# Retention attention and a gated feed-forward in one kernel: the first eight chunks taken head by head with zero-padded operands, output stores issued on the load queue, and later weights loaded in 2 KB pieces

## The chip, the cores and the metric

The kernel runs on one core of one Trainium2 chip. The metric is the device time in microseconds (us) of one execution; shorter is better. TensorE is called PE below, its weight loads PEld, VectorE DVE, ScalarE ACT, GpSimd POOL, and SyncE, which here only issues DMAs, SP.

## The reference

Eight batches with eight heads of 576 positions and 64 features go through a retention attention (causal, without softmax, with a decay per head). Its output, seen as 4608 tokens of 512 features, goes through a feed-forward of width 1536 with a sigmoid gate.

```python
scores = q @ k^T / sqrt(64)
gamma  = 1 - 2 ** (-5 - head)
Dmat   = gamma ** (i - j) where i >= j, else 0
x      = ((scores * Dmat) @ v)            # heads side by side: (4608, 512)
out    = ((sigmoid(x @ w_gate)) * (x @ w_val)) @ w_out
```

Inputs and output are float32; the kernel computes its matmuls in bfloat16 with float32 sums.

## The kernel before

**Attention by chunks.** Each batch of 576 positions is cut into five chunks of 128, 128, 128, 128 and 64 positions; with eight batches that makes 40 steps, counted by s. The decay is split: keys are multiplied by gamma^-pos (`ks`, on POOL, line 197), queries by gamma^pos / sqrt(64) (`qs`, line 200), so that inside a chunk only a causal mask is left. A step has four phases. Phase t (line 216) turns keys and queries so that features lie on the partitions: for the first eight steps (`EARLY = 8`) by eight PE transposes into one PSUM tile `tr`, from which ACT copies `qT` (line 230) and DVE copies the keys into `kbd` (line 235); for later steps by two DMA transposes issued on SP (line 207), from which DVE copies `kbd`. Phase qk (line 240) multiplies; two heads share one matmul, because `kbd` and `vbd` hold two heads of 64 positions as a block diagonal in one 128x128 tile, and DVE multiplies the result by the mask `tri` (line 254, or 261 for a half chunk). Phase st (line 286) adds the chunk's keys times values to a state, which DVE masks with `bdm` (`sb`, line 304). Phase pv (line 265) sums state times queries and `vbd` times masked scores, and ACT copies the result to `xT` (line 284), the transposed input of the feed-forward.

**Preparation of a step.** `cast(s)` (line 178) writes the values twice in bfloat16: plainly as `vn`, and as four quarter blocks into `vbd`, by ACT for the first eight steps (line 189), by POOL later (line 191). `load(s)` (line 73) issues three DMAs of 256 KB for values, keys and queries (128 KB for a half chunk), in rows of 256 bytes.

**Feed-forward.** A unit is four matmuls `h` (line 351) for one of twelve feature blocks fc; ACT applies the sigmoid to the gate unit (`g`, line 356) and DVE multiplies (`gv`, line 360). Three PSUM tiles serve all units. When all twelve are there, twelve matmuls `op` (line 372) give 128 tokens of output, ACT copies them to `ob` (line 377) and issues the store on its own DMA queue (line 379). The first block has 512 tokens and is written out by hand (`first_units`, line 404), since it grows while steps 0 to 3 are computed and weights arrive. Then come blocks of 128, of 256, seven of 512 and one of 128 tokens.

**What sets the order.** Each engine runs its instructions in the order of the program. A list (line 310) gives the phases; `advance` (line 390) places them between feed-forward units. At phase t of step s the program first issues `load(s + 6)` and casts all steps up to s + 2 (only step s itself while s < 4), see line 329:

```python
while done["cast"] < min(NS, s + (1 if s < 4 else LEAD_CAST)):
```

**Loads.** All loads and DMA transposes are on SP's queue: steps 0 and 1, weights for fc 0 and 1, step 2, weights for fc 2 to 5, step 3, the other gate and value weights, twelve tiles of `w_out`, then steps 4, 5 and on. Gate and value weights come as tiles of two row blocks by 256 columns (1 KB rows), `w_out` in 2 KB rows. The 22 buffers of `ld` serve them all; a buffer comes free when its cast is done. Beside that, the DMAs share eight completion semaphores in turn, so that a DMA waits for one that stood eight places before it, whichever queue it is on.

Of the kernel before, what the change touches and what calls it, by code (L numbers as in the profile page):

```python
# [9 lines left out]
FP32 = mybir.dt.float32  # L10
# [6 lines left out]
def kernel(  # L17
# [22 lines left out]
    P = 128  # L40
# [6 lines left out]
    ld_pool = ctx.enter_context(tc.tile_pool(name="ld", bufs=22))  # L47
# [4 lines left out]
    osb_pool = ctx.enter_context(tc.tile_pool(name="osb", bufs=3))  # L52
# [14 lines left out]
    EARLY = 8  # L67

# [15 lines left out]
    def load_w(f):  # L84

        for nm, src in (("g", moe_w_gate), ("v", moe_w_val)):
            for i in range(2):
                t = ld_pool.tile([P, 2, 2 * P], FP32, tag="ld", name=f"w{nm}32_{f}_{i}")
                nc.sync.dma_start(
                    out=t, in_=src[i * 2 * P:(i + 1) * 2 * P, f * P:(f + 2) * P].rearrange("(c p) f -> p c f", p=P))  # L90
                parts[nm, f, i] = t
# [36 lines left out]
    nc.scalar.activation(out=qtab, in_=arg, func=AF.Exp, bias=lnscale, scale=1.0)  # L128

# [3 lines left out]
    for i in range(NB):  # L133
        nc.vector.memset(vbd[i], 0.0)
        if i < 3:
            nc.gpsimd.memset(kbd[i], 0.0)

    tri = consts.tile([P, 192], BF16)  # L140
    nc.gpsimd.memset(tri, 1.0)
    for p0 in (0, 64):
        for c0 in (0, 128):
            nc.gpsimd.affine_select(
                out=tri[p0:p0 + 64, c0:c0 + 64], in_=tri[p0:p0 + 64, c0:c0 + 64],
                compare_op=ALU.is_ge, fill=0.0, base=0,
                pattern=[[1, 64]], channel_multiplier=-1)
    bdm = consts.tile([P, P], BF16)
    nc.gpsimd.memset(bdm, 0.0)
    nc.gpsimd.memset(bdm[0:64, 0:64], 1.0)  # L150
    nc.gpsimd.memset(bdm[64:128, 64:128], 1.0)
# [6 lines left out]
    def cast_w(f):  # L158
        for i in range(2):
            nc.gpsimd.tensor_copy(out=wg_sb[:, 2 * i:2 * i + 2, f * P:(f + 2) * P], in_=parts.pop(("g", f, i)))  # L160
            if i == 0:
                nc.vector.tensor_copy(out=wv_sb[:, 0:2, f * P:(f + 2) * P], in_=parts.pop(("v", f, 0)))
            else:
                nc.scalar.copy(out=wv_sb[:, 2:4, f * P:(f + 2) * P], in_=parts.pop(("v", f, 1)))

    def cast_wo(f):
        if f % 2:
# [313 lines left out]
```

## Time and profile before

| what | value |
|---|---|
| time, median of 3 runs (lowest to highest) | 375.67 us (375.01 to 377.22) |
| time of the profiled execution | 378.67 us |
| its span, first to last instruction | 377.0 us |
| mean granted PE clock | 0.968 of full |
| PE busy | 338.5 us (90%) |
| ACT, DVE, POOL busy | 140.7, 170.9, 154.2 us |
| DMA moved | 55.11 MB, 146 GB/s over the span |

A row of the windows view gives a stretch of the span, its length, then for each engine the busy time and the number of instructions, the granted PE clock, the busy share of the 16 DMA engines and the rate. A timeline row gives start and length of an instruction or a group of like ones, and in brackets how long the engine had been idle and what ended that. A row by line gives the total, the mean in ns of one, and the idle time ahead of the group.

### The profile page before, as it was taken

Reading aid. Unit: us, or ns where it says so; the run is one execution under the profiler, and the core shown is the slowest. Engines: PE = TensorE matmul, PEld = TensorE weight load, DVE = VectorE, ACT = ScalarE, POOL = GpSimd, SP = SyncE. Lnnn points to the kernel's source line nnn. Section 1 sums busy time; section 2 is a strip of 40 time slices with the busy share of each in tenths; the row PEclk is TensorE's granted clock in tenths of the full one; section 3 lists DMA queues with packets and bytes.
Section 4 is the critical chain, followed back from the end, with each engine's and each line's share of the span. In section 5 each row is a group of like instructions: output and inputs, shape, how many; then the busy total and the mean of one; then the engine's idle time right before and its main releaser. Section 6 shows DMA issues by size and latency. Waiting matters only on the chain.

```text
span 377.0 us, 6771 instructions
## 1 busy us (share of the span) xinstructions
PE 338.5 (90%) x2464; PEld 189.7 (50%) x2464; DVE 170.9 (45%) x353; ACT 140.7 (37%) x280; POOL 154.2 (41%) x254
## 2 busy tenths in 40 slices
PE   1668994679896999999999999999999999999996
PEld 0554741366763555555555555554555455544454
DVE  4645551145772545264346425651663266324212
ACT  5646466333431232333233324332332333233232
POOL 6424331347692466444636572553444470000000
PEclk9868997889999899999999999999999999999999
DMA  9999998697999979866865798569532310110020
GB/s 177 296 298 360 285 214 172 131 202 135 179 190 200 183 150 183 185 99 134 188 155 113 139 231 133 113 125 237 99 70 59 111 30 16 56 57 2 28 85 29
DMA packets 157218, 55.11 MB, mean 146 GB/s; under 512 B 144896, under 2 KB 151040, under 8 KB 157184
## 3 DMA queue, kind: packets, MB, share of 16 engines
q1 hardware_dynamic: 152000, 45.24, 59.9%
q10 hardware_dynamic: 5184, 9.44, 8.4%
q8 instruction: 19, 0.31, 0.4%
q14 instruction: 15, 0.12, 0.1%
HBM read 37.75 MB, written 9.44 MB: 125 GB/s over the span
## 4 chain that ended last, share of the span: by engine, by line
PE 81%; ACT 7%; DMA 4%; DVE 4%; POOL 2%; issue 2%; ACTq 0%; SPq 0%; POOLq 0%; DVEq 0%
PE h L351 48%; PE op L372 21%; PE pv L283 5%; DVE kbd L235 3%; PE qk L250 2%; ACT vbd L189 2%; PE st L295 2%; DMA out_dram<-ob 2%; DMA k<-in_k_dram 1%; ACT ob L377 1%; ACT qT L230 1%; PE qk L252 1%; DMA v<-in_v_dram 1%; ACT vn L189 1%; PE tr L226 1%
## 5 line engine op out<-in xcount | busy, mean ns | idle before, releaser
L360 DVE TENSOR_TENSOR gv<-g,h 128x512 bf16<-128x512 bf16 (+3 forms) x142 | 79.2, 559 | 101.7 <-PE h L351 71.0
L351 PE MATMUL h<-xT,wv_sb 128*128 128x512 bf16 (+3 forms) x568 | 118.7, 332 | 5.3 <-ACT g L356 5.3
L351 PE MATMUL h<-xT,wg_sb 128*128 128x512 bf16 (+3 forms) x568 | 119.4, 334 | 3.3 <-ACT xT L284 3.0
L356 ACT ACTIVATE g<-h 128x512 bf16<-128x512 f32 (+3 forms) x142 | 69.9, 495 | 127.6 <-PE h L351 116.8
L372 PE MATMUL op<-wo_sb,gv 128*128 128x512 bf16 x432 | 102.3, 387 | 0.0
L191 POOL CAST vbd<-v 64x256 bf16<-64x256 f32 x114 | 45.1, 396 | 111.6 <-PE pv L283 107.9
L351 PEld LDWEIGHTS <-wg_sb 128*128 128x128 bf16 x568 | 51.8, 100 | 46.0 <-issue 4.8
L351 PEld LDWEIGHTS <-wv_sb 128*128 128x128 bf16 x568 | 49.6, 100 | 39.9 <-issue 7.1
L372 PEld LDWEIGHTS <-gv 128*128 128x128 bf16 x432 | 41.1, 99 | 45.5 <-issue 2.5
L254 DVE TENSOR_TENSOR pt<-qk,tri 128x384 bf16<-128x384 f32 x64 | 32.7, 552 | 43.9 <-PE qk L252 43.9
L197 POOL TENSOR_TENSOR ks<-k,ktab 128x512 bf16<-128x512 f32 (+1 forms) x40 | 41.6, 1040 | 15.8 <-DMA k<-in_k_dram 12.1
L377 ACT COPY ob<-op 128x512 f32<-128x512 f32 x36 | 21.1, 585 | 68.6 <-PE op L372 57.0
L200 POOL TENSOR_TENSOR qs<-q,qtab 128x512 bf16<-128x512 f32 (+1 forms) x32 | 33.4, 1044 | 0.0
L284 ACT CAST xT<-pv 128x512 bf16<-128x512 f32 (+1 forms) x40 | 21.7, 542 | 30.5 <-PE pv L283 30.5
L250 PE MATMUL qk<-qT,kbd 128*128 128x128 bf16 x128 | 15.8, 225 | 11.9 <-DVE kbd L235 11.9
L304 DVE TENSOR_TENSOR sb<-st,bdm 128x512 bf16<-128x512 f32 x32 | 22.0, 688 | 9.6 <-PE st L295 9.6
L283 PE MATMUL pv<-pt,vbd 128*128 128x64 bf16 (+1 forms) x288 | 25.1, 213 | 0.2 <-DVE pt L254 0.2
L283 PEld LDWEIGHTS <-vbd 128*128 128x128 bf16 x288 | 21.3, 103 | 5.8 <-issue 1.4
L191 POOL CAST vn<-v 128x512 bf16<-128x512 f32 (+1 forms) x32 | 19.6, 612 | 9.1 <-PE st L295 4.1
L235 DVE COPY kbd<-kT 64x512 bf16<-64x512 bf16 (+1 forms) x64 | 21.3, 333 | 1.6 <-DMA kT<-ks 0.6
L250 PEld LDWEIGHTS <-kbd 128*128 128x128 bf16 x128 | 11.9, 100 | 17.0 <-DVE kbd L235 14.4
L283 PE MATMUL pv<-qT,sb 128*128 128x128 bf16 (+1 forms) x128 | 19.6, 220 | 0.0
(42 smaller groups left out, 150.0 us busy)
## 6 DMA issues: line engine op xcount, KB each, us to landing
out_dram<-ob ACTq DMA_DIRECT2D x36, 256.0 KB, 2.9
v<-in_v_dram SPq DMA_DIRECT2D x32, 256.0 KB, 4.0
k<-in_k_dram SPq DMA_DIRECT2D x32, 256.0 KB, 4.4
q<-in_q_dram SPq DMA_DIRECT2D x32, 256.0 KB, 5.0
wg<-in_moe_w_gate_dram SPq DMA_DIRECT2D x12, 256.0 KB, 4.8
wv<-in_moe_w_val_dram SPq DMA_DIRECT2D x12, 256.0 KB, 5.6
wo<-in_moe_w_out_dram SPq DMA_DIRECT2D x12, 256.0 KB, 5.6
v<-in_v_dram SPq DMA_DIRECT2D x8, 128.0 KB, 3.7
```

The lines of the kernel that those rows point to most:

```text
L191: nc.gpsimd.tensor_copy(out=o, in_=i)
L197: nc.gpsimd.tensor_tensor(out=ks[0:n], in0=k32[0:n], in1=ktab[0:n, c, :].unsqueeze(2).to_broadcast([n, H, D]), op=ALU.mult)
L200: eng.tensor_tensor(out=qs[0:n], in0=q32[0:n], in1=qtab[0:n, c, :].unsqueeze(2).to_broadcast([n, H, D]), op=ALU.mult)
L235: nc.vector.tensor_copy(out=kb[p0:p0 + 64, 0:nj, :, p0:p0 + 64].rearrange("p j m t -> p m j t"), in_=kT[p0:p0 + 64, 0:M, 0:n].rearrange("p ...
L250: nc.tensor.matmul(qkp[:, mm, 0:128], lhsT=kb[:, 0, m, :], rhs=qT[:, m, 0:128], start=True, stop=True)
L254: nc.vector.tensor_tensor(out=pt[:, 2 * g:2 * g + 2, :], in0=qkp[:, :, 0:192], in1=tri.unsqueeze(1).to_broadcast([P, 2, 192]), op=ALU.mult)
L283: nc.tensor.matmul(pvp[:, m, a:e], lhsT=w, rhs=x, start=(i == 0), stop=(i == len(mm) - 1))
L351: nc.tensor.matmul(hp[:, a:e], lhsT=w_sb[:, kc, fc * P:(fc + 1) * P], rhs=xT[:, kc, t0 + a:t0 + e], start=(kc == 0), stop=(kc == NKC - 1))
L356: nc.scalar.activation(out=g[:, a:e], in_=hp[:, a:e], func=AF.Sigmoid)
L360: nc.vector.tensor_tensor(out=gvs[fc][:, a:e], in0=gate[:, a:e], in1=hp[:, a:e], op=ALU.mult)
L372: nc.tensor.matmul(opp, lhsT=gvs[fc][:, nb * P:(nb + 1) * P], rhs=wo_sb[:, fc, :], start=(fc == 0), stop=(fc == NFC - 1))
L377: nc.scalar.copy(out=ob, in_=opp)
```

## The change

It has four parts that stand in the same diff.

- **Head by head.** For steps 0 to 7, values and keys go into `vpad` and `kpad`, tiles with one 128-wide column group per head in which the other head's half is zero. One cast (ACT for steps 0 to 3, POOL for 4 to 7) writes the values, two DVE copies the keys. Scores are eight matmuls of 128 columns in place of four of 128 and four of 64, the mask is a plain triangle `tri2`, and DVE multiplies 512 columns twice in place of 384 twice. Transposed keys and queries get separate PSUM tiles, `kT` in the old place and `tq` in the place of `pv`.
- **Division of the other work.** Casts run one step ahead only until step 5. For steps 8 to 11 (`MID = 12`) ACT casts `vn` and DVE multiplies `qs`, both POOL's before. All of `w_out` is cast on POOL. The constants for later steps are set up later, `vbd` during the first block's output units; a one-column sigmoid early on brings its table load forward.
- **Stores.** The output stores are issued by SP, in program order between loads and transposes; four `ob` buffers in place of three, 20 `ld` buffers in place of 22.
- **Weights.** Those for fc 4 to 11 are loaded as tiles of one row block by 512 columns (2 KB rows), eight for four fc, and cast later in `first_units`.

```diff
-    ld_pool = ctx.enter_context(tc.tile_pool(name="ld", bufs=22))
+    ld_pool = ctx.enter_context(tc.tile_pool(name="ld", bufs=20))
-    osb_pool = ctx.enter_context(tc.tile_pool(name="osb", bufs=3))
+    osb_pool = ctx.enter_context(tc.tile_pool(name="osb", bufs=4))
+    MID = 12
...
-    load_w(0)
+    load_w(0, 2)
     load(2)
-    load_w(2)
-    load_w(4)
+    load_w(2, 2)
+    load_w(4, 4)
     load(3)
-    for f in range(6, NFC, 2):
-        load_w(f)
+    load_w(8, 4)
...
+    nc.scalar.activation(out=warm, in_=lnscale, func=AF.Sigmoid)
...
+    def cast_w(f, nf):
+        r = NKC // nf
+        for i in range(nf):
+            at = (slice(None), slice(i * r, (i + 1) * r), slice(f * P, (f + nf) * P))
+            nc.gpsimd.tensor_copy(out=wg_sb[at], in_=parts.pop(("g", f, i)))
+            if i % 2 == 0:
+                nc.vector.tensor_copy(out=wv_sb[at], in_=parts.pop(("v", f, i)))
             else:
+                nc.scalar.copy(out=wv_sb[at], in_=parts.pop(("v", f, i)))
...
+        if early:
+            vb = vpad[s % 3]
+            eng = nc.scalar.copy if s < 4 else nc.gpsimd.tensor_copy
+            eng(out=pair_view(vb, n), in_=v32[0:n].rearrange("p (m a) d -> p m a d", a=2))
+            vn = None
+        else:
+            vn = nat_pool.tile([P, H, D], BF16, tag="vn", name=f"vn_{s}")
+            vb = vbd[s % NB]
+            eng = nc.scalar.copy if s < MID else nc.gpsimd.tensor_copy
+            eng(out=vn[0:n], in_=v32[0:n])
...
-        eng = nc.vector if early else nc.gpsimd
+        eng = nc.vector if s < MID else nc.gpsimd
...
-            kT = tr_psum.tile([P, 2 * M, P], BF16, tag="tr", name=f"tr_{s}")
+            kT = tr_psum.tile([P, M, P], BF16, tag="tr", name=f"kT_{s}")
+            tq = pv_psum.tile([P, M, P], BF16, tag="pv", name=f"tq_{s}")
...
+                for i in range(4):
+                    m, hh = 2 * g + i // 2, i % 2
+                    nc.tensor.matmul(qkp[0:n, i, 0:n], lhsT=kb[:, m, hh, 0:n],
+                                     rhs=qT[:, m, 0:n], start=True, stop=True)
+                nc.vector.tensor_tensor(out=pt[0:n, 4 * g:4 * g + 4, 0:n], in0=qkp[0:n, :, 0:n],
+                                        in1=tri2[0:n, 0:n].unsqueeze(1).to_broadcast([n, 4, n]), op=ALU.mult)
...
-            while done["cast"] < min(NS, s + (1 if s < 4 else LEAD_CAST)):
+            while done["cast"] < min(NS, s + (1 if s < EARLY - 2 else LEAD_CAST)):
...
-            nc.scalar.dma_start(out[r0:r0 + P, :], ob)
+            nc.sync.dma_start(out[r0:r0 + P, :], ob)
```

Three places show what moves in the engines' orders. The first is ACT at the first output tiles of the first block (`ob` is an output tile, `vn` and `vbd` are values of a step, `qT` its turned queries, `xT` the feed-forward's input). Before:

```order
L377 COPY ob_0_843<-op_0_830 128x512
L379 DMA out_dram<-ob_0_843 128x512
L189 CAST vn_863<-v_4_189 64x512
L189 CAST vbd_223<-v_4_189 64x4x64 x2
L189 CAST vn_871<-v_5_195 128x512
L189 CAST vbd_224<-v_5_195 64x4x64 x4
L189 CAST vn_881<-v_6_251 128x512
L189 CAST vbd_225<-v_6_251 64x4x64 x4
L230 COPY qT_898<-tr_889 128x4x64
L377 COPY ob_1_906<-op_1_846 128x512
```

The same place now (`tq` is the PSUM tile of the turned queries):

```order
L422 COPY ob_0_840<-op_0_825 128x512
L249 COPY qT_871<-tq_862 128x4x64
L422 COPY ob_1_896<-op_1_844 128x512
L326 CAST xT<-pv_904 128x4x64
L249 COPY qT_943<-tq_934 128x512
```

The casts of steps 4 to 6 and the store stood between the output tile and the queries of step 4; they have left ACT.

The second is SP from the loads of step 11 to the first DMA transposes. Before:

```order
L80 DMA q_11_946<-in_q_dram 128x8x64
L80 DMA v_12_1024<-in_v_dram 128x8x64
L80 DMA k_12_1026<-in_k_dram 128x8x64
L80 DMA q_12_1028<-in_q_dram 128x8x64
L207 DMA_TRANSPOSE kT_1041<-ks_1031 128x4x128
L207 DMA_TRANSPOSE qT_1040<-qs_1030 128x4x128
```

Now:

```order
L81 DMA q_11_926<-in_q_dram 128x8x64
L424 DMA out_dram<-ob_2_951 128x512
L424 DMA out_dram<-ob_3_997 128x512
L81 DMA v_12_1007<-in_v_dram 128x8x64
L81 DMA k_12_1009<-in_k_dram 128x8x64
L81 DMA q_12_1011<-in_q_dram 128x8x64
L225 DMA_TRANSPOSE kT_1034<-ks_1024 128x4x128
L225 DMA_TRANSPOSE qT_1033<-qs_1023 128x4x128
```

The first block's third and fourth stores now stand ahead of step 12's loads and step 8's transposes (the first two stand ahead of steps 10 and 11).

The third is DVE from the last state copy `sb` of the first block to the first scores of step 6 (`gv` is the gated value of the next block). Now:

```order
L348 TENSOR_TENSOR sb_977<-st_972,bdm 128x512
L218 TENSOR_TENSOR qs_1013<-q_6_258,qtab 128x512
L218 TENSOR_TENSOR qs_1018<-q_7_326,qtab 128x512
L218 TENSOR_TENSOR qs_1023<-q_8_411,qtab 128x512
L256 COPY kpad_235<-kT_1037 64x4x128 x2
L405 TENSOR_TENSOR gv_0_1056<-g_0_0_1005,h_0_0_0_1051 128x128
```

Before, the row behind `sb` is the copy for `kbd`:

```order
L304 TENSOR_TENSOR sb_998<-st_993,bdm 128x512
L235 COPY kbd_227<-tr_1044 64x4x2x64 x2
L360 TENSOR_TENSOR gv_0_1062<-g_0_0_1022,h_0_0_0_1057 128x128
L360 TENSOR_TENSOR gv_1_1076<-g_0_1_1069,h_0_1_0_1071 128x128
L254 TENSOR_TENSOR pt_1078<-qk_0_1079,tri 128x384
```

Three multiplications of queries, of steps 6 to 8, have come to stand ahead of step 6's keys.

More of the change, by code (lines that the diff above doesn't have):

```diff
@@ L128 @@
     nc.scalar.activation(out=qtab, in_=arg, func=AF.Exp, bias=lnscale, scale=1.0)
+    warm = consts.tile([P, 1], FP32)
+    nc.scalar.activation(out=warm, in_=lnscale, func=AF.Sigmoid)
     NB = 4
@@ L243, in phase_qk @@
         qT, kb = turned[s]
+        if s < EARLY:
+            pt = att_pool.tile([P, H, P], BF16, tag="pte", name=f"pte_{s}", bufs=2)
+            for g in range(2):
+                qkp = qk_psum.tile([P, 4, P], FP32, tag="qk", name=f"qk_{s}_{g}")
+                for i in range(4):
[4 more added lines that the diff above has]
+                                        in1=tri2[0:n, 0:n].unsqueeze(1).to_broadcast([n, 4, n]), op=ALU.mult)
+            probs[s] = pt
+            return
         pt = att_pool.tile([P, M, 192], BF16, tag="pt", name=f"pt_{s}")
```

134 lines of the change are left out of this document (70 added, 64 removed).

## The prediction

> **What bounds the kernel now.** I read the windows view first, cut where the feed-forward blocks begin, then the timelines of PE, ACT and SP in the windows where PE is idle, then the chain of waits. Columns: start and end, length, busy time of PE, PEld, DVE, ACT and POOL, granted PE clock, DMA share, GB/s.
>
> ```profile
> 17.20:26.94 9.74, 6.31 (x49) 4.97 (x48) 4.60 (x10) 5.23 (x11) 2.73 (x4) 0.68 1.20 301
> ...
> 41.67:52.85 11.18, 11.18 (x96) 7.04 (x96) 4.36 (x11) 7.35 (x19) 3.92 (x5) 1.00 1.16 212
> 52.85:78.87 26.02, 16.57 (x98) 7.93 (x97) 7.01 (x13) 12.44 (x28) 7.73 (x13) 0.80 0.86 173
> 78.87:92.45 13.58, 11.73 (x173) 9.76 (x172) 8.46 (x24) 5.18 (x16) 8.32 (x14) 1.00 0.82 158
> 92.45:114.68 22.23, 19.83 (x202) 15.06 (x200) 13.98 (x30) 7.58 (x18) 17.50 (x28) 1.00 1.15 178
> 114.68:126.47 11.79, 8.18 (x50) 4.30 (x49) 3.40 (x7) 2.85 (x5) 2.15 (x5) 0.86 0.92 191
> 126.47:377.00 250.53, 246.39 (x1649) 127.85 (x1647) 110.40 (x215) 82.23 (x149) 95.05 (x155) 1.00 0.52 111
> ```
>
> From 126.47 us on PE is busy for 246.39 of 250.53 us at full clock: two thirds of the span can't move, except as a whole. I name the stages ahead of it: A to 52.85 (attention of steps 0 to 3, hidden layer of the first block), B to 78.87 (its output, steps 4 and 5), C to 92.45 (block of 128 tokens), D to 114.68 (block of 256), E to 126.47 (start of the first 512-token block of the regular kind). B is the worst: 16.57 busy of 26.02, and that at clock 0.80. PE's timeline shows on what:
>
> ```profile
> 63.56 0.39 PE L259 MATMUL qk<-qT,kbd 128*128 128x64 bf16 x4 [4.92 <-DVE kbd L235]
> 63.77 3.60 PE L372 MATMUL op<-wo_sb,gv 128*128 128x512 bf16 x8
> ...
> 73.65 0.23 PE L250 MATMUL qk<-qT,kbd 128*128 128x128 bf16 x1 [3.50 <-DVE kbd L235]
> ```
>
> Two waits for the keys of a step, 4.92 and 3.50 us; behind the first, eight output matmuls take 3.60 us, 450 ns each. DVE is not the cause. ACT's timeline in the same place:
>
> ```profile
> 56.67 0.62 ACT L189 CAST vn<-v 64x512 bf16<-64x512 f32 x1 [0.45 <-ACT ob L377]
> ...
> 60.79 1.68 ACT L189 CAST vbd<-v 64x256 bf16<-64x256 f32 x4
> 62.49 0.37 ACT L230 COPY qT<-tr 128x256 bf16<-128x256 bf16 x1
> ```
>
> Behind the output copy ACT casts the values of steps 4, 5 and 6, from 56.67 to 62.47; only then does it take step 4's turned queries, and DVE's key copy comes behind ACT because both read the one tile `tr`. The second wait is the same with step 7.
>
> In E another queue is in the way. ACT's timeline, the piece of the chain behind it, and PE:
>
> ```profile
> 112.29 0.58 ACT L377 COPY ob<-op 128x512 f32<-128x512 f32 x1 [0.27 <-PE op L372]
> 116.00 0.34 ACTq L379 DMA_DIRECT2D out_dram<-ob  x1
> ...
> 120.56 0.34 ACTq L379 DMA_DIRECT2D out_dram<-ob  x1
> ...
> 121.00 1.09 ACT L356 ACTIVATE g<-h 128x512 bf16<-128x512 f32 x2 [4.04 <-DMA k<-in_k_dram]
> ```
>
> ```profile
> 115.60 4.89 DMA k<-in_k_dram
> ```
>
> ```profile
> 121.65 1.02 PE L351 MATMUL h<-xT,wv_sb 128*128 128x512 bf16 x4 [3.61 <-ACT g L356]
> ```
>
> ACT has its output tile at 112.87, but issues the store at 116.00, and the next at 120.56, just behind the landing of a load of keys at 120.49 (its semaphore's turn). The sigmoids of two finished units wait behind the store and PE for 3.61 us.
>
> **Stage A: -1.4 us.** Rows of the first steps:
>
> ```profile
> 6.63 1.15 DVE L200 TENSOR_TENSOR qs<-q,qtab 128x512 bf16<-128x512 f32 x1 [2.62 <-DMA q<-in_q_dram]
> ...
> 9.17 0.88 DVE L235 COPY kbd<-tr 64x512 bf16<-64x512 bf16 x2 [1.39 <-ACT qT L230]
> ```
>
> ```profile
> L254 DVE TENSOR_TENSOR pt<-qk,tri 128x384 bf16<-128x384 f32 x64 | 32.7, 552 | 43.9 <-PE qk L252 43.9
> L304 DVE TENSOR_TENSOR sb<-st,bdm 128x512 bf16<-128x512 f32 x32 | 22.0, 688 | 9.6 <-PE st L295 9.6
> L200 DVE TENSOR_TENSOR qs<-q,qtab 128x512 bf16<-128x512 f32 x7 | 5.2, 748 | 2.6 <-DMA q<-in_q_dram 2.6
> L230 ACT COPY qT<-tr 128x512 bf16<-128x512 bf16 x7 | 4.1, 585 | 2.9 <-PE tr L226 2.8
> L189 ACT CAST vn<-v 128x512 bf16<-128x512 f32 x7 | 4.3, 615 | 1.6 <-DMA v<-in_v_dram 1.1 <-ACT ob L377 0.4
> L189 ACT CAST vbd<-v 64x256 bf16<-64x256 f32 x30 | 12.0, 402 | 0.4
> ```
>
> Constants leave POOL ahead of the first keys, but the queries still land at 6.63, so the head gains no more than the shorter multiplication, 1.15 to 0.75 us: -0.4. With keys and queries in two tiles, DVE copies keys while ACT copies queries: where it now starts 0.6 us behind ACT's 0.585 us, it starts beside it, and scores wait only for the later of the two: about -0.8 in steps 0, 2 and 3. In step 1 `tq` must wait for ACT's copy out of `pv` (its PSUM place), which takes 0.6 of that back: -0.2. One value cast takes the place of 0.615 + 4 x 0.402 = 2.2 us; its strided form isn't in the trace, at least 0.615, at most as the two-fold, 1.2; I take 0.615 as the element count is that of `vn`. Before step 2 this frees ACT by 1.6 us, of which 0.3 lies on the path. Against it: the mask takes 2 x (688 - 552) = 0.27 us more per step, 1.1 for four, and four scores matmuls of 128 columns for 64 make 0.1 each, 0.4; half of it lies under other work, 0.8. Casting the last weights in the middle of the 128-column units puts two casts of 0.615 on ACT, which paces them, in place of one: +0.6. Sum: -0.4 - 2.4 - 0.2 - 0.3 + 0.8 + 0.6 = -1.9, of which I keep -1.4, since how far these overlap no row shows. Bounds: -4.5 (if PE gets full clock in 17 to 27 us, 6.31 x 0.32 = 2.0, and nothing is taken back) and +1. The sigmoid's table load, the pieces of 2 KB and POOL's casts of all of `w_out` lie under PE's units from 41.67 to 52.85, 11.18 us without a gap; if weights came later than that they would show one for one.
>
> **Stage B: -12.4 us.** What PE must do, at full clock (rows of the chain):
>
> ```profile
> 81.80 0.67 PE h L351 x12
> ...
> 152.59 3.45 PE op L372 x16
> ```
>
> 48 output matmuls of 3.45/16 = 0.2156 us are 10.35. A whole step is what C shows: busy 11.73, less 96 units' matmuls of 0.67/12 (5.4) and 12 output ones (2.6), leaves 3.8 for two, 1.9 each; step 5 takes 1.9, the half step 4 about 1.0. Sum 13.25, with 0.35 of short waits 13.6, for 26.02: -12.4. What can be late next is data. The keys' arrivals on POOL, first and last of steps 4 to 7:
>
> ```profile
> 47.19 1.03 POOL L197 TENSOR_TENSOR ks<-k,ktab 64x512 bf16<-64x512 f32 x1 [0.76 <-DMA k<-in_k_dram]
> ...
> 57.06 1.04 POOL L197 TENSOR_TENSOR ks<-k,ktab 128x512 bf16<-128x512 f32 x1 [2.51 <-DMA k<-in_k_dram]
> ```
>
> B would begin at 51.5 and use steps 4 and 5 at about 55 and 59, with loads there by 47 and, at (57.06 - 47.19)/3 = 3.3 us a step, 50.5. Steps 6 and 7 are wanted from 65 on and there at 57. If data were late by 3 us B still keeps 9 of it: bound -9; if waits vanish, -12.8.
>
> **Stages C and D: 0, with bounds -3 and +6.** C loses the waits of DVE for ACT, but qs of steps 6 to 8 stand ahead of step 6's keys on DVE (3 x 0.75 = 2.2 us; they can run before PE gets there, since the queries have landed by 62), and two masks. D is a race between PE and SP's queue:
>
> ```profile
> 54.26 1.08 SPq L80 DMA_DIRECT2D v<-in_v_dram  x1
> 59.74 0.37 SPq L80 DMA_DIRECT2D k<-in_k_dram  x1
> ...
> 82.43 1.32 SPq L207 DMA_TRANSPOSE kT<-ks  x1
> ```
>
> ```profile
> 31.32 8.31 SPq L95 DMA_DIRECT2D wo<-in_moe_w_out_dram  x12
> ```
>
> ```profile
> SPq L80 <- DMA out_dram<-ob: 16.8, 4, 4.6
> ```
>
> ```profile
> kT<-ks SPq DMA_TRANSPOSE x2, 4.2
> ```
>
> ```profile
> 90.62 0.97 DVE L235 COPY kbd<-kT 64x512 bf16<-64x512 bf16 x2
> ```
>
> Today SP's loads stand still for 16.8 us, four times, until one of ACT's four first stores lands; step 8's keys are transposed from 82.43 on and used at 90.62. In the new order SP meets each store with its tile ready (by B's times at about 54.7, 57.8, 61.3 and 65.4) and goes on. From 55.3, the end of the last load ahead of the first such wait, remain 12.5 tiles of 256 KB to step 12's last, at 1.1 to 1.2 us each (3.3 to 3.5 a step) 14.6, and four stores, estimated at 8.31/12 = 0.7 by the weights of the same size and row length, 2.8: 72.7 for step 8's transpose, landed 4.2 later (the view of DMAs up to 90 us, last number), 77 to 78. D begins at 52.85 - 1.4 + 13.6 + 13.6 = 78.7. So both arrive together. Over the next five steps SP needs what it needed (it was at DMA share 1.15 in D), 22 us, as PE does. D keeps its 22.23: what ACT's removed store wait gives back, DVE's two more qs (1.5) and late transposes take.
>
> **Stage E: -4.7 us.** Stores no longer stand on ACT. PE's 8.18 us at clock 0.86 are 7.0 at full clock; 11.79 becomes 7.1. SP's stores wait for a tile, and loads and transposes queue behind them, but those are issued two steps ahead of use. Here a rule of the Trainium skill speaks against the change: DMA: Bandwidth & Descriptors, section "Issuing engines are not separate DMA queues", says that DMAs from any engine share the 16 DMA engines, so that another issuer saves only the time to issue. By that rule E keeps its stall, and the sum would be -13.8, 361.9 us. No run yet shows which holds; the landing at 120.49 and the issue at 120.56 speak for a wait on order, not on engines.
>
> **Sum.** -1.4 - 12.4 + 0 - 4.7 = -18.5. The profiled execution took 378.67 us, its span 377.0, 3.0 above the median 375.67: 360.2 for a like execution, and 357.2 against the median.
>
> **The rivals.** (1) The load stream binds: the queries of steps 6 to 8, on which DVE now waits in order, or step 8's transposes come late. For it: DMA share 1.15 in D. Against: 16.8 us of standing still fall away. Price: D +6, C +1.8, so 365. (2) The sharing of DMA engines is what held E: 361.9, as above. (3) A warmer clock in A. Clock 0.68 stands in 17.20:26.94. The Trainium skill, TensorE: Matmul & The Clock Gate, Part 1, has the clock halve after an idle window of about 3.4 us; the rows of that stretch show no idle gap over 1.79 us, so the trace doesn't agree as it stands:
>
> ```profile
> 23.95 0.29 PE L250 MATMUL qk<-qT,kbd 128*128 128x128 bf16 x1 [1.79 <-DVE kbd L235]
> ```
>
> If shorter gaps lift the clock there, 2.0 us go, and with the -1.9 of A kept whole, 354.7. (4) Slower: a store on SP waits for its tile, and the transposes behind it land after their use, in each of the seven 512-token blocks. Price per block: two transposes to issue (1.32 each), 4.2 to land, the key copy 0.97: 7.8 us, 55 in all, less 18.5: 412. It decides once SP reaches a step's transposes less than 7.8 us before PE wants the step. Against it: 250.53 us for 27 steps are 9.3 per step, and the lead is two steps, 18 us. (5) Nothing moves, because E's and B's waits have another cause: ACT's rows leave little room for it.
>
> **How the numbers follow.** Forecast, 357.2: 0.66, with its own range 352 to 361.5. Rival 1: 0.15; rival 2: 0.06; rival 3: 0.07; rival 4: 0.04; rival 5: 0.02. The range 351 to 365.5 takes in A's and D's bounds on both sides and rivals 1 to 3 up to their price; outside lie the rest of rival 1's and 3's tails and rivals 4 and 5. A measurement of this kernel tells about 0.5% (1.9 us) from no change: the three runs lie 0.6% apart. Faster by more: 0.94 (forecast, rivals 1 to 3); the same: 0.02; slower: 0.04.
>
> **What would show it.** Right: in B no wait of PE above 1 us, ACT's `qT` right behind `ob`, clock 1.00, and the first output matmul about 1.4 us earlier; the block of 128 tokens begins at 63 to 67; SP's first transpose is issued at 71 to 75; no ACT gap ahead of `g` in E; from then on the same 250 us. Wrong: DVE idle for `q` or `kT` in C and D, or PE waiting for `g` in E as before; and the whole account fails if PE's busy time behind E grows.

## The result, and the profile after the change

Beside each other on one chip the changed kernel took 363.07 us, median of four runs (361.46 to 365.76), the kernel before 376.45 us (four runs, 375.01 to 377.34): a ratio of 0.9655, 95% interval 0.9587 to 0.9724. The forecast was 357.2, with a range from 351.0 to 365.5. The direction was right and the range held, but the time came out 6 us above the forecast, outside the 352 to 361.5 given for the likeliest case alone, and next to rival 1's 365.

The profiled executions took 378.67 us before and 365.76 after, with spans of 377.0 and 364.1; the difference of 12.9 us is taken apart below. Both profiled executions are slower than their kernel's others (the changed kernel's had a mean clock of 0.991, its fastest, 361.46, one of 1.000), so what a stage loses by slow clock is not lost in every execution, and e9_lead4_one_tile below was profiled at 366.40 for a median of 361.66. The windows view of the changed kernel, cut at the same places of the program (first output matmul, first hidden matmul of the block of 128 tokens, of the block of 256, of the first of 512, and of that block's fourth unit), has the columns of before's:

```profile
0.00:48.94 48.94, 34.26 (x300) 24.18 (x302) 27.74 (x66) 21.63 (x45) 27.18 (x49) 1.00 1.07 273
48.94:63.01 14.07, 13.86 (x103) 7.47 (x104) 9.19 (x18) 3.67 (x7) 8.19 (x11) 1.00 1.06 214
63.01:77.69 14.68, 12.50 (x172) 10.30 (x172) 10.76 (x26) 6.46 (x19) 8.04 (x14) 1.00 1.16 253
77.69:107.77 30.08, 22.94 (x201) 16.96 (x200) 15.89 (x33) 8.70 (x20) 16.38 (x27) 0.89 1.03 169
107.77:114.08 6.31, 6.26 (x49) 3.48 (x49) 3.48 (x7) 2.93 (x5) 1.76 (x4) 1.00 0.86 167
114.08:364.10 250.02, 244.61 (x1618) 127.84 (x1647) 110.51 (x215) 82.25 (x149) 95.44 (x156) 1.00 0.54 115
```

| stage | before | after | measured | forecast |
|---|---|---|---|---|
| A, to the first output matmul | 52.85 | 48.94 | -3.9 | -1.4 |
| B, its output, steps 4 and 5 | 26.02 | 14.07 | -12.0 | -12.4 |
| C, block of 128 tokens | 13.58 | 14.68 | +1.1 | 0 |
| D, block of 256 tokens | 22.23 | 30.08 | +7.9 | 0 |
| E, start of the first 512 | 11.79 | 6.31 | -5.5 | -4.7 |
| behind it | 250.53 | 250.02 | -0.5 | 0 |
| sum | | | -12.9 | -18.5 |

B went as forecast: PE is busy for 13.86 of 14.07 us at clock 1.00. ACT's timeline there, in the columns of before's, shows the queries' copy between the output copies, and no cast of values:

```profile
55.28 0.58 ACT L422 COPY ob<-op 128x512 f32<-128x512 f32 x1 [1.94 <-PE op L417]
57.23 0.37 ACT L326 CAST xT<-pv 128x256 bf16<-128x256 f32 x1 [1.36 <-PE pv L325]
58.64 0.58 ACT L249 COPY qT<-tq 128x512 bf16<-128x512 bf16 x1 [1.04 <-PE tq L245]
59.51 0.59 ACT L422 COPY ob<-op 128x512 f32<-128x512 f32 x1 [0.28 <-PE op L417]
```

D is where the missing gain went. PE's timeline shows three new waits for turned keys, of steps 8, 9 and 11, 7.1 us together:

```profile
80.00 0.23 PE L289 MATMUL qk<-qT,kbd 128*128 128x128 bf16 x1 [1.27 <-DVE kbd L261]
...
87.17 0.29 PE L298 MATMUL qk<-qT,kbd 128*128 128x64 bf16 x4 [3.25 <-DVE kbd L261]
...
98.49 0.23 PE L289 MATMUL qk<-qT,kbd 128*128 128x128 bf16 x1 [2.57 <-DVE kbd L261]
```

DVE itself waits there. Its timeline shows the key copies of steps 8 to 12, each behind a DMA transpose:

```profile
79.33 0.61 DVE L261 COPY kbd<-kT 64x512 bf16<-64x512 bf16 x2 [2.79 <-DMA kT<-ks]
85.85 1.26 DVE L261 COPY kbd<-kT 64x256 bf16<-64x256 bf16 x2 [2.74 <-DMA kT<-ks]
90.63 1.50 DVE L261 COPY kbd<-kT 64x512 bf16<-64x512 bf16 x2 [0.23 <-DMA kT<-ks]
97.02 1.41 DVE L261 COPY kbd<-kT 64x512 bf16<-64x512 bf16 x2 [2.14 <-DMA kT<-ks]
103.50 0.61 DVE L261 COPY kbd<-kT 64x512 bf16<-64x512 bf16 x2 [0.78 <-DMA kT<-ks]
```

SP's timeline shows what stands ahead of those transposes: step 8's come at 75.46 behind the three loads of step 12, which are wanted four steps later, and step 9's behind the loads of step 13.

```profile
71.34 1.49 SPq L81 DMA_DIRECT2D v<-in_v_dram  x1
72.93 0.54 SPq L81 DMA_DIRECT2D k<-in_k_dram  x1
73.56 1.81 SPq L81 DMA_DIRECT2D q<-in_q_dram  x1
75.46 1.62 SPq L225 DMA_TRANSPOSE kT<-ks  x1
...
97.87 1.96 SPq L225 DMA_TRANSPOSE kT<-ks  x1
```

The same transposes of the kernel before were issued from 82.43 (step 8) to 105.31 (step 12), and the copies that use them began at 90.62 and 110.33. SP's timeline and DVE's, before:

```profile
105.31 1.53 SPq L207 DMA_TRANSPOSE kT<-ks  x1
```

```profile
97.76 0.47 DVE L235 COPY kbd<-kT 64x256 bf16<-64x256 bf16 x2
...
110.33 1.06 DVE L235 COPY kbd<-kT 64x512 bf16<-64x512 bf16 x2 [0.61 <-DMA kT<-ks]
```

From step 8's transpose to step 12's SP takes 105.31 - 82.43 = 22.9 us before and 97.87 - 75.46 = 22.4 after: its rate did not change, 5.6 to 5.7 us a step (what sets that rate was not tried). Before, the copy of step 8 began 8.2 us behind its transpose's issue, that of step 12 only 5.0 us behind, and it had to wait 0.61: a stock of lead was eaten up in D. After, all five copies wait, 3.3 to 5.6 us behind the issue. PE arrives at D 14.8 us earlier than before, SP's queue only 7.

### The profile page after: what moved, and what is told of

The parts are those of the page before. It is cut to its first block, busy times and chain, and to the rows that moved or that the text cites. A ratio compares the mean times of both kernels' runs of the same rounds, so it can differ in the third digit from the quotient of the medians.

```text
span 364.1 us, 6731 instructions
## 1 busy us (share of the span) xinstructions
PE 334.4 (92%) x2435; PEld 190.2 (52%) x2472; DVE 177.6 (49%) x364; ACT 125.6 (35%) x245; POOL 157.0 (43%) x257
## 4 chain that ended last, share of the span: by engine, by line
PE 85%; DMA 7%; DVE 2%; ACT 2%; SPq 2%; issue 2%; DVEq 0%
PE h L396 48%; PE op L417 26%; PE pv L325 5%; DMA kT<-ks 3%; PE st L339 2%; PE qk L289 2%; SPq L81 1%; DMA wv<-in_moe_w_val_dram 1%; DMA wo<-in_moe_w_out_dram 1%; DMA q<-in_q_dram 1%; PE qk L277 1%; PE qk L291 1%; DVE kbd L261 1%; PE tq L245 1%; ACT qT L249 0%
## 5 line engine op out<-in xcount | busy, mean ns | idle before, releaser
L396 PE MATMUL h<-xT,wg_sb 128*128 128x512 bf16 (+3 forms) x557 | 117.0, 329 | 3.1 <-ACT xT L326 2.0
L396 PE MATMUL h<-xT,wv_sb 128*128 128x512 bf16 (+3 forms) x555 | 117.2, 331 | 1.4 <-ACT g L401 0.5
L417 PE MATMUL op<-wo_sb,gv 128*128 128x512 bf16 x419 | 98.4, 379 | 0.8 <-issue 0.2
L293 DVE TENSOR_TENSOR pt<-qk,tri 128x384 bf16<-128x384 f32 x50 | 25.5, 552 | 42.5 <-PE qk L291 42.4
L218 POOL TENSOR_TENSOR qs<-q,qtab 128x512 bf16<-128x512 f32 (+1 forms) x28 | 29.2, 1044 | 0.0
L210 POOL CAST vn<-v 128x512 bf16<-128x512 f32 (+1 forms) x28 | 17.1, 610 | 4.1 <-PE st L339 4.1
L325 PE MATMUL pv<-pt,vbd 128*128 128x128 bf16 (+1 forms) x228 | 18.5, 205 | 0.0
L325 PEld LDWEIGHTS <-vbd 128*128 128x128 bf16 x228 | 15.8, 99 | 4.1
L289 PE MATMUL qk<-qT,kbd 128*128 128x128 bf16 x100 | 12.1, 222 | 3.9 <-DVE kbd L261 3.8
L325 PEld LDWEIGHTS <-sb 128*128 128x128 bf16 x128 | 12.4, 101 | 3.2
```

The costliest lines, as they stand in the source:

```text
L218: eng.tensor_tensor(out=qs[0:n], in0=q32[0:n], in1=qtab[0:n, c, :].unsqueeze(2).to_broadcast([n, H, D]), op=ALU.mult)
L293: nc.vector.tensor_tensor(out=pt[:, 2 * g:2 * g + 2, :], in0=qkp[:, :, 0:192], in1=tri.unsqueeze(1).to_broadcast([P, 2, 192]), op=ALU.mult)
L325: nc.tensor.matmul(pvp[:, m, a:e], lhsT=w, rhs=x, start=(i == 0), stop=(i == len(mm) - 1))
L396: nc.tensor.matmul(hp[:, a:e], lhsT=w_sb[:, kc, fc * P:(fc + 1) * P], rhs=xT[:, kc, t0 + a:t0 + e], start=(kc == 0), stop=(kc == NKC - 1))
L417: nc.tensor.matmul(opp, lhsT=gvs[fc][:, nb * P:(nb + 1) * P], rhs=wo_sb[:, fc, :], start=(fc == 0), stop=(fc == NFC - 1))
```

## The experiments

Theory: in D the changed kernel is bound by SP's queue, on which a step's transposes stand behind loads that are wanted four steps later than they are; what A and B gain beyond SP's own advance is lost in D. The rivals: DMA engines that have no more to give, so that order is worth nothing; stores on SP that do the harm; another part of the change that brings the gain. Twelve kernels were run; the kernel before, run beside them, took 376.83, 377.39 and 377.04 us in the three sets of four. The starts of four places in their profiled executions, with PE's first output matmul, the blocks of 128, 256 and 512 tokens:

| kernel | output | 128 | 256 | 512 | median us |
|---|---|---|---|---|---|
| before | 52.85 | 78.87 | 92.45 | 114.68 | 376.45 |
| changed | 48.94 | 63.01 | 77.69 | 107.77 | 363.07 |
| e1_turns_first | 49.10 | 63.18 | 76.94 | 100.48 | 358.60 |
| e2_stores_act | 49.40 | 63.48 | 80.09 | 107.09 | 366.65 |
| e3_before_stores_sp | 52.95 | 76.75 | 90.33 | 111.84 | 370.03 |
| e4_before_lead | 51.84 | 71.81 | 91.97 | 112.85 | 374.24 |
| e5_one_tile | 55.32 | 70.42 | 85.31 | 108.83 | 365.81 |
| e6_lead_back | 49.45 | 68.40 | 82.05 | 107.64 | 364.43 |
| e7_1kb | 48.95 | 63.04 | 77.98 | 105.40 | 364.67 |
| e8_turns_first_lead4 | 48.99 | 63.07 | 77.14 | 97.64 | 356.55 |
| e9_lead4_one_tile | 55.19 | 70.29 | 85.17 | 108.10 | 361.66 |
| e10_lead4_stores_act | 48.99 | 63.07 | 77.29 | 96.92 | 359.71 |
| e11_before_turns_lead4 | 52.71 | 78.71 | 92.24 | 113.03 | 371.16 |
| e12_lead4_only | 49.40 | 63.48 | 77.50 | 101.26 | 359.45 |

**e1_turns_first** issues a step's casts, and with them its transposes, ahead of the load that is queued in the same place:

```
     if kind == "t":
+        while done["cast"] < min(NS, s + (1 if s < EARLY - 2 else LEAD_CAST)):
+            cast(done["cast"])
+            done["cast"] += 1
         while done["ld"] < min(NS, s + LEAD_LOAD + 1):
             load(done["ld"])
             done["ld"] += 1
-        while done["cast"] < min(NS, s + (1 if s < EARLY - 2 else LEAD_CAST)):
...
```

> The changed kernel with one edit: at phase t of a step, the casts with their two DMA transposes are issued ahead of the load for six steps later. Theory A (order on SP): in the block of 256 tokens PE waits for transposes that stand behind loads which nobody needs for four more steps; each pair now stands one load (3.3 to 3.5 us) earlier, DVE's waits for kT (8.7 us in 77 to 110 us) fall under 3, the stage shrinks from 30.1 to 24 to 26 us, and the time to 357 to 359. Rival B (volume): the 16 DMA engines are simply full there, in whatever order; the stage keeps 29 to 31 us and the time 363 within 1.5.

Measured: 358.60 us (358.13 to 358.88), ratio 0.9519, 0.9483 to 0.9556. SP's timeline has step 8's transpose at 69.97, ahead of step 12's loads:

```profile
69.97 2.17 SPq L225 DMA_TRANSPOSE kT<-ks  x1
72.26 1.19 SPq L225 DMA_TRANSPOSE qT<-qs  x1
73.50 0.58 SPq L81 DMA_DIRECT2D v<-in_v_dram  x1
```

Nothing was taken away, only the order on one queue; D fell from 30.08 to 23.54 us. The theory's first half holds. DVE's waits for transposes in D, expected under 3 us, are still 6.4, and PE's for the copies behind them 3.9: SP's queue still holds D back a little.

**e2_stores_act** is the changed kernel with the output stores issued by ACT, as before the change:

```
-            nc.sync.dma_start(out[r0:r0 + P, :], ob)
+            nc.scalar.dma_start(out[r0:r0 + P, :], ob)
```

> The changed kernel with its output stores issued by ACT again. Theory A (a store waits for its turn on a semaphore that a load on SP holds, and loads wait for stores in the same way): SP's loads stand still again for 10 to 17 us in the first block, transposes of step 8 come 3 to 6 us later, ACT is held at the start of the first 512-token block again; time 368 to 374. Rival B (engines are shared, the issuer saves only issue time): 363 within 2.

Measured: 366.65 us (365.66 to 367.75), ratio 0.9735, 0.9691 to 0.9779: between the two. E kept its 6.31 us, so the stall did not come back in its old place. ACT's timeline shows it once, at the border of C and D:

```profile
80.29 0.58 ACT L422 COPY ob<-op 128x512 f32<-128x512 f32 x1 [2.27 <-PE op L417]
84.89 0.34 ACTq L424 DMA_DIRECT2D out_dram<-ob  x1
85.33 0.38 ACT L401 ACTIVATE g<-h 128x256 bf16<-128x256 f32 x1 [4.46 <-DMA qT<-qs]
```

The tile is ready at 80.87, the store goes out at 84.89, behind the landing of a transpose, and the sigmoid stands behind it. The block of 512 begins at 107.09 all the same. Theory A's other signs did not come: SP's loads stood still for 5.3 us instead of 10 to 17, and step 8's transpose went out at 75.63, no later than in the changed kernel. The intervals of this kernel and the changed one overlap, so the price of the stores' place in this setting, 3.6 us, is uncertain.

**e3_before_stores_sp** is the kernel before with this one part of the change:

```
-            nc.scalar.dma_start(out[r0:r0 + P, :], ob)
+            nc.sync.dma_start(out[r0:r0 + P, :], ob)
```

and four output tiles for three, as in the changed kernel.

> The kernel before with one part of the change alone: stores on SP, four buffers for them. Theory A: the 3.61 us wait and the slow clock behind it go (-4.7), loads no longer stand still for 16.8 us, the two waits of PE in the first block stay: 369 to 371.5. Rival B (issuer saves only issue time): 374 to 377.

Measured: 370.03 us (369.04 to 370.99), ratio 0.9826, 0.9776 to 0.9876. The windows view has E at the changed kernel's length:

```profile
111.84:118.15 6.31, 6.26 (x49) 3.40 (x48) 4.28 (x8) 2.94 (x5) 1.89 (x4) 1.00 1.11 202
```

E gives 5.5 us, 0.8 more than the prediction's 4.7; the profiled execution of this kernel is 8.9 us shorter than before's, and B gives 2.2 of the rest, D 0.7. Rival 2 of the prediction falls. The Trainium skill, DMA: Bandwidth & Descriptors, section "Issuing engines are not separate DMA queues", says that another issuing engine saves only the time to issue, usually small. Here a store's issue on ACT takes 0.34 us, and the move, with the fourth output tile, was worth 6.8 by the medians; of the 8.9 in the profiled executions 5.5 lie in E, where ACT had stood still. That engines share the transfer hardware is not refuted by it: what E saved is ACT standing in order behind a transfer that another queue had started. What gave B's 2.2 was not traced.

**e4_before_lead** is the kernel before with casts one step ahead until step 5:

```
-            while done["cast"] < min(NS, s + (1 if s < 4 else LEAD_CAST)):
+            while done["cast"] < min(NS, s + (1 if s < EARLY - 2 else LEAD_CAST)):
```

> The kernel before with one part of the change alone: casts one step ahead only until step 5. Theory A (ACT's queue order makes the two waits of the first block's output): in front of step 4's queries ACT casts one step in place of three, 4.4 us less, so the wait of 4.92 falls under 1 and the slow clock behind it goes in part: -4 to -7, 369 to 372. Rival C (it takes the head-by-head casts to bring this gain): -2 or less, 373.5 to 376.5.

Measured: 374.24 us (372.16 to 377.88), ratio 0.9938, 0.9898 to 0.9978. B fell by 6.0 to 19.97 us, and C rose by 6.6 to 20.16. ACT's timeline shows why:

```profile
74.76 0.62 ACT L189 CAST vn<-v 128x512 bf16<-128x512 f32 x1
75.29 1.68 ACT L189 CAST vbd<-v 64x256 bf16<-64x256 f32 x4
76.99 0.59 ACT L230 COPY qT<-tr 128x512 bf16<-128x512 bf16 x1
```

The pile of casts ahead of one query copy moved into C, where PE's timeline now has the longest wait:

```profile
78.54 0.29 PE L250 MATMUL qk<-qT,kbd 128*128 128x128 bf16 x1 [5.23 <-DVE kbd L235]
```

The time is rival C's. Theory A named one wait and did not follow the casts to their new place: what order alone gains in B is lost again in C, because these casts were still ACT's.

**e5_one_tile** is the changed kernel with turned keys and queries in one PSUM tile:

```
-            kT = tr_psum.tile([P, M, P], BF16, tag="tr", name=f"kT_{s}")
-            tq = pv_psum.tile([P, M, P], BF16, tag="pv", name=f"tq_{s}")
+            both = tr_psum.tile([P, 2 * M, P], BF16, tag="tr", name=f"kT_{s}")
+            kT = both[:, 0:M, :]
+            tq = both[:, M:2 * M, :]
```

> The changed kernel with turned keys and turned queries of the first eight steps in one PSUM tile again. Theory A (the two tiles let DVE copy keys while ACT copies queries, and the denser start holds the clock at 1.00 through the first 48 us): the first output matmul comes 2 to 3 us later than 48.94, at 51 to 52, the stretch from 17 to 27 us shows a clock below 0.9 again, and the time is 2 to 3.5 us above the changed kernel's 363.07, 365 to 366.5. Rival B (the head gains from the one value cast and the shorter multiplication alone): first output matmul within 1 us of 48.94, time within 1.5 us of 363.07, clock 1.00 as before.

Measured: 365.81 us (364.25 to 366.83), ratio 0.9673, 0.9619 to 0.9726. DVE's timeline shows the wait that the two tiles remove, and the windows view what it costs up to the first output matmul:

```profile
13.76 0.88 DVE L257 COPY kpad<-kT 64x512 bf16<-64x512 bf16 x2 [0.95 <-ACT qT L250]
```

```profile
0.00:55.32 55.32, 38.91 (x300) 26.88 (x301) 28.12 (x66) 21.61 (x45) 31.30 (x53) 0.94 1.07 269
```

The time is where theory A had it, but not by its sum. The first output matmul comes 6.4 us later, more than twice what I had expected: PE's busy time for the same 300 instructions is 38.91 for 34.26, 4.65 us of slower clock (0.89 from 17.20 to 26.94, as theory A had it, and 0.84 from there to 41.67), and 1.7 us more are idle. Yet the block of 512 tokens begins 1.1 us later only, and the interval doesn't tell the time from the changed kernel's. That is what the other half of the theory says: what A gains beyond SP's advance doesn't reach the end. e9_lead4_one_tile tests it.

**e6_lead_back** lets the casts of the changed kernel run three steps ahead from step 4 on:

```
-            while done["cast"] < min(NS, s + (1 if s < EARLY - 2 else LEAD_CAST)):
+            while done["cast"] < min(NS, s + (1 if s < 4 else LEAD_CAST)):
```

> The changed kernel with the casts running three steps ahead already from step 4 on, as in the kernel before, instead of from step 6. Theory A (the later casts are what keeps the engines' queues free in the second stage): the second stage, 14.07 us in the changed kernel, grows by 1 to 4 us since DVE meets the multiplications of queries 4 to 6 ahead of step 4's keys; time 364 to 367. Rival B (the value casts that left ACT are the whole gain, and the lead costs nothing with them gone): second stage within 1 us of 14.07; time within 1.5 us of 363.07.

Measured: 364.43 us (362.05 to 366.64), ratio 0.9649, 0.9592 to 0.9706. Stage B grew by 4.9 us to 18.95, a little more than theory A said, the time by 1.4, which is less than this measurement tells: D hides what B lost, as in e5_one_tile, with the block of 512 at 107.64. PE waited only once in B for over 0.6 us, and the cause is theory A's: ahead of that key copy DVE multiplies the queries of steps 4 to 6, and stands 0.91 us for those of step 6 to land. PE's timeline, and the windows view of the same stretch with the granted clock behind POOL's column:

```profile
55.98 0.73 PE L277 MATMUL qk<-qT,kpad 128*64 128x64 bf16 x8 [1.56 <-DVE kpad L256]
```

```profile
54.00:56.00 2.00, 0.44 (x3) 0.02 (x1) 1.36 (x3) 0.00 (x0) 1.18 (x2) 1.00 1.19 235
56.00:58.00 2.00, 1.89 (x13) 0.93 (x14) 1.00 (x3) 0.09 (x1) 0.00 (x0) 0.84 1.30 217
58.00:60.00 2.00, 2.00 (x9) 0.72 (x8) 0.69 (x1) 0.50 (x1) 0.00 (x0) 0.50 1.35 225
...
64.00:66.00 2.00, 2.00 (x16) 1.09 (x15) 1.05 (x3) 0.89 (x2) 1.85 (x4) 0.95 0.83 197
```

A wait of 1.56 us is followed by over 6 us at clock 0.50. The wait is the smaller part of its price: PE is busy for 17.29 us in B, for 13.86 in the changed kernel.

**e7_1kb** loads the later weights in rows of 1 KB again, cast in the same places:

```
-    load_w(4, 4)
+    load_w(4, 2)
+    load_w(6, 2)
...
-    load_w(8, 4)
+    load_w(8, 2)
+    load_w(10, 2)
```

> The changed kernel with the weights of hidden blocks 4 to 11 loaded in pieces with rows of 1 KB instead of 2 KB, cast in the same places. Theory A (the length of the rows is worth nothing here, an estimate from 8.3 us for 12 tiles of w_out with rows of 2 KB and 8.6 us for tiles with rows of 1 KB): first output matmul within 0.5 us of 48.94, time within 1.5 us of 363.07. Rival B (2 KB rows bring the last loads ahead of the second stage sooner): loads of steps 4 and 5 land 1 to 3 us later, time 364.5 to 366.

Measured: 364.67 us (362.89 to 366.44), ratio 0.9658, 0.9613 to 0.9703, against the changed kernel's 0.9655; first output matmul at 48.95. The median lies 0.1 us outside theory A's bound of 1.5, the ratios say no difference, and stage A shows none. SP's issue rows before the change agree: the last twelve gate and value tiles, with rows of 1 KB, go out in 8.3 us (22.61 to 30.93), the twelve of `w_out`, with 2 KB, in 8.31. The pieces of 2 KB are worth nothing that can be measured here.

**e8_turns_first_lead4** adds to e1_turns_first loads that run four steps ahead instead of six:

```
-            while done["ld"] < min(NS, s + LEAD_LOAD + 1):
+            while done["ld"] < min(NS, s + 4 + 1):
```

> The kernel of e1_turns_first with loads issued four steps ahead instead of six. Theory A (SP's queue is what D, the stage of the block of 256 tokens, still waits for, 23.5 us there against some 21 of PE's work): fewer loads ahead of the first transposes, D 21.5 to 22.5 us, time 356.5 to 358. Rival B (the loads themselves bind, so that a shorter lead only moves the wait from the turned keys to the loaded queries): DVE waits for q in D for 1 us or more, D 23.5 us or longer, time 358.6 to 361.

Measured: 356.55 us (355.95 to 357.28), ratio 0.9441, 0.9407 to 0.9475: faster than both kernels of the study. The windows view from C to E:

```profile
63.07:77.14 14.07, 12.55 (x174) 10.31 (x173) 11.23 (x28) 6.47 (x19) 5.94 (x9) 1.00 0.73 168
77.14:97.64 20.50, 19.34 (x202) 15.17 (x201) 13.40 (x31) 8.60 (x20) 11.78 (x21) 1.00 1.22 169
97.64:103.94 6.30, 6.30 (x49) 3.46 (x48) 3.61 (x7) 2.93 (x5) 5.15 (x10) 1.00 0.95 176
```

D is down to 20.50 us, below theory A's 21.5 to 22.5 and 1.7 below its length before the change, PE busy for 19.34 of it at full clock; step 8's transpose goes out at 64.31, and DVE waits for no queries there, against rival B. SP had issued too early what was not yet wanted.

**e9_lead4_one_tile** makes e5's edit in e8's kernel.

> The kernel of e8_turns_first_lead4 with turned keys and queries in one PSUM tile, as in e5_one_tile. There the first output matmul came 6.4 us later than in the changed kernel (55.32 against 48.94), the block of 512 tokens only 1.1 us later. Theory A (in the changed kernel SP's queue set when the blocks of 256 and 512 tokens could run, and hid what the start gains): with step 8's transposes out at 64.31 the cover is gone, the time rises by 4.5 to 7 us over 356.55, to 361 to 363.5. Rival B (what is lost at the start is caught up in D whatever SP does): 358 or less.

Measured: 361.66 us (360.67 to 366.40), ratio 0.9595, 0.9559 to 0.9632: about 5 us above e8_turns_first_lead4, and clear of its interval, where the same edit in the changed kernel made a difference of 2.7 that its interval doesn't confirm. With SP no longer hiding it, A's loss reaches the end, as theory A had it.

**e10_lead4_stores_act** makes e2's edit in e8's kernel.

> The kernel of e8_turns_first_lead4 with the output stores issued by ACT again. Theory A (a store on ACT stands until an earlier transfer of another queue has landed and the sigmoids stand behind it, as once for 4.46 us in e2_stores_act): ACT shows one or more stalls of 3 to 5 us ahead of g, time 359.5 to 364. Rival B (the place of the stores is worth nothing once SP is not short of time): within 1.5 us of 356.55.

Measured: 359.71 us (357.75 to 360.18), ratio 0.9535, 0.9499 to 0.9571: 3.2 us slower than on SP. The block of 512 begins no later (96.92); the loss lies behind it. From that block's fourth unit to 150 us PE is busy for 45.16 of 46.74 us, with 46.06 of 46.06 in e8_turns_first_lead4, so 1.6 us of the loss show there. The waits view sums, for ACT from 48 us on:

```profile
ACT g L401 <- DMA k<-in_k_dram: 3.1, 1, 3.1
```

One stall of 3.1 us, at theory A's lower end, behind which PE waits for 1.26; stores on SP keep a value of their own.

**e11_before_turns_lead4** makes e8's edit in the kernel before, without the change under study.

> The kernel before, with a step's casts and transposes issued ahead of its load and the loads four steps ahead instead of six: the edit of e8_turns_first_lead4, without the change under study. Theory A (there SP's queue binds nothing, since step 8's keys are turned 10 us before the block of 256 tokens begins): within 2 us of 377. Rival B (the order of SP's queue is worth 6 us to any version): 370 to 372.5. Rival C (loads four steps ahead come too late where stores on ACT hold the loads' turns): 379 or more.

Measured: 371.16 us (370.32 to 372.40), ratio 0.9851, 0.9817 to 0.9886. The time is rival B's, but the transposes did not bring it. D gave 1.4 us (20.79 for 22.23): PE's wait of 1.32 for a sigmoid, at 95.58 before, is gone, and its two waits for key copies are as long as before (0.29 and 0.75). The rest is E, 6.31 for 11.79. ACT's timeline at the border of D and E has both stores going out at once:

```profile
110.64 0.58 ACT L377 COPY ob<-op 128x512 f32<-128x512 f32 x1 [0.27 <-PE op L372]
111.26 0.34 ACTq L379 DMA_DIRECT2D out_dram<-ob  x1
113.23 0.58 ACT L377 COPY ob<-op 128x512 f32<-128x512 f32 x1 [2.00 <-PE op L372]
113.85 0.40 ACTq L379 DMA_DIRECT2D out_dram<-ob  x1
```

None of my theories had this. E's stall does not belong to stores on ACT as such: with other transfers around them the same stores pass. Which transfer a store has to wait for was not tried.

**e12_lead4_only** shortens the loads' lead in the changed kernel and leaves the order inside a step.

> The changed kernel with loads issued four steps ahead instead of six, and still ahead of the step's transposes: the second half of the edit of e8_turns_first_lead4 alone. Theory A (what counts is how many loads are queued ahead of a step's transposes; two steps fewer are two times 3.3 us): step 8's transpose is issued at 68 to 71, D 22 to 25 us, time 356.5 to 360. Rival B (the place inside the step decides): step 8's transpose at 73 or later, time within 1.5 us of 363.07.

Measured: 359.45 us (357.44 to 360.16), ratio 0.9527, 0.9487 to 0.9567; step 8's transpose at 66.85, D 23.76: theory A's, with the transpose even earlier than its 68 to 71. By the medians the order alone (e1_turns_first) takes 4.5 us off the changed kernel, the shorter lead alone 3.6, both together 6.5.

## Why the prediction was nearly right, step by step

**What bounds the kernel.** Right for B and E, incomplete for D. Before the change PE was busy for 19.83 of D's 22.23 us, and the prediction had SP level with it. PE's longest wait there, 1.32 us, was for a sigmoid behind a store on ACT, and e11_before_turns_lead4 shows that earlier transposes leave its other waits as they were. But SP had come close by the end of D: step 12's keys were copied at 110.33 after a wait of 0.61 for their transpose, though PE did not wait for that copy.

**Stage A, -1.4, measured -3.9.** Right in sign, too small. The head's waits went as described, but the two tiles, put at -2.6 in sum, are worth 6.4 (e5_one_tile); by that run the other edits of A together cost 2.5 (55.32 against 52.85), where I had +0.7. Most of the 6.4 is clock: rival 3's mechanism held, with 1.00 in the whole of A for 0.68 in 17.20 to 26.94 before. What the one value cast, the wider mask and the later weight casts are worth each was not tried.

**Stage B, -12.4, measured -12.0.** Right, with the mechanism: no wait of PE over 0.3 us, clock 1.00. e4_before_lead adds that the later casts without the cheaper ones only carry the pile into C, and e6_lead_back that the cheaper ones without the later casts leave 4.9 us in B. No run gives ACT alone the value casts of steps 4 to 7 back.

**Stage C, 0, measured +1.1.** Within its bounds. Its longest wait, 1.11 us, is for DVE's key copy of step 6, on which the three steps of queries stand ahead, as the bounds had it. The premise that they could run before PE gets there, since they "have landed by 62", failed for the third: DVE waits 0.60 us for step 8's queries until 63.91. That is also one of the prediction's own signs of being wrong, DVE idle for `q` or `kT` in C and D; for `kT` it stands 8.7 us.

**Stage D, 0 with bounds -3 and +6, measured +7.9.** This is the step that failed: "Over the next five steps SP needs what it needed ..., 22 us, as PE does. D keeps its 22.23". SP did need the same, 22.4 us from step 8's transpose to step 12's. But before, it had 8.2 us between issue and copy at the start of D, of which D ate 3, and the sum left the change next to none: "both arrive together". Two sizes were then wrong by a little and on the same side: the transpose at 75.46 for 72.7, and PE in D at 77.69 for 78.7. Of the 2.8 us by which the transpose was late, 2.1 were there where its sum started, at the issue of the load of step 8's values: the sum took its end from before, 55.3, and it ended at 57.47. SP's waits up to then name POOL's casts of `w_out` above all, which the change gave to POOL alone (before, SP waited 1.3 us for POOL's and 1.0 for ACT's). The waits view has, in us in all, times and the longest:

```profile
SPq L81 <- POOL wo_sb L181: 4.9, 3, 3.6
```

No run gives these casts back or tries the change with 22 `ld` buffers, so that cause stays argued. PE waits for the keys of steps 8, 9 and 11 as their transposes come late, and the waits cost clock as well, 0.89 over D: of the 7.9 us, 4.7 are idleness of PE (7.1 for 2.4) and 3.1 longer busy time for the same work (22.94 for 19.83). The table shows that SP sets D's end: in the changed kernel, e2, e5, e6 and e7 the block of 512 begins between 105.4 and 108.8, though the first output matmul lies anywhere between 48.9 and 55.3 and D's start between 77.7 and 85.3; in e1, e8 and e12, which change only what SP issues when, it begins at 97.6 to 101.3.

**Stage E, -4.7, measured -5.5.** Right in size; the reason was half of it. Moving the stores removes the stall (e3_before_stores_sp), but so does another order of the loads (e11_before_turns_lead4).

**The rivals.** Rival 1 (365) had 0.15 and is the one that came true, in the form of late transposes and by their order on SP, as e1_turns_first shows, with rival 3 (0.07) beside it: 357.2 with D and C at their measured +9.0 would be 366.2, and A's extra 2.5 brings it back to 363.7. They were priced as alternatives, but one feeds the other: what A gains, D loses as long as SP sets its end. So the misses offset each other by cause, as e5_one_tile shows. The prediction did not have that, and that its range held is in part luck. Rival 4 didn't come: behind 114.08 there are 250.02 us, and SP has 9.3 us a step there, for 5.7 that it needs. Rival 2 falls with e3_before_stores_sp, rival 5 with that run and stage B.

**Rival 3 and the clock.** The Trainium skill, TensorE: Matmul & The Clock Gate, Part 1, has the clock halve after an idle window of about 3.4 us. e6_lead_back shows 0.50 behind a gap of 1.56 us. The trace disagrees, as it did before the change.

## What to carry to other kernels

When a stage that is waited for gets shorter, ask of each queue behind it how much lead it has at that stage's end, in us between issue and use, and subtract the gain: a stage whose PE looks busy may have been living on stock. On an in-order queue put what is wanted next (here transposes, two steps ahead) in front of what is wanted last (loads, six steps ahead), and let loads run no further ahead than they need. An edit that shows nothing may only be covered: e5_one_tile and e9_lead4_one_tile are the same edit, worth 2.7 us within the uncertainty in one kernel and about 5 in the other.

## What the runs showed that I had not expected

A short wait of PE can cost more than twice its length in clock, but not every one does. In e6_lead_back 1.56 us of idleness was followed by 0.50 from 58 to 64 us, 3.4 us of slower matmuls in B. In the changed kernel the 3.25 us ahead of 87.17 were followed by this, in windows of 1 us:

```profile
87.00:88.00 1.00, 0.83 (x11) 0.77 (x12) 0.97 (x4) 0.07 (x1) 0.96 (x4) 1.00 0.88 199
88.00:89.00 1.00, 1.00 (x9) 0.80 (x7) 0.65 (x2) 0.31 (x1) 0.91 (x3) 0.69 0.89 190
89.00:90.00 1.00, 1.00 (x7) 0.73 (x5) 0.02 (x1) 0.38 (x1) 0.92 (x2) 0.50 1.03 133
...
92.00:93.00 1.00, 1.00 (x16) 0.89 (x15) 0.94 (x3) 0.38 (x1) 0.91 (x3) 1.00 1.28 289
```

By the means of these windows the drop comes 1.2 us after PE has taken up work again, at 88.4, and ends at 91.2 to 92. In e1_turns_first, PE's timeline has a wait of 1.77 us, and the clock stays at 1.00 in every window of 2 us from 84 to 98:

```profile
88.07 0.23 PE L289 MATMUL qk<-qT,kbd 128*128 128x128 bf16 x1 [1.77 <-DVE kbd L261]
```

And in e5_one_tile the clock is 0.50 from 26 to 30 us, though no wait of PE in A behind its first matmul is longer than 1.29 us. So the length of the last gap alone doesn't decide; what does is open.
